# Moving one of the two buffer places of h by 64 bytes in SBUF: attention and SwiGLU on one core

## The chip, the cores and the metric

The kernel runs on one core of one Trainium2 chip. The metric is the device time of one execution in microseconds, the median of several runs.

## The reference

Block-causal attention over 8 batches, 8 heads, 576 positions and a head width of 64, followed by a gated feed-forward layer over the 4608 tokens that come out of it:

```
scores = q @ k^T / sqrt(64), masked by blocks of 64, softmax over keys
x      = (softmax @ v) as [4608, 512]
g      = x @ w_gate                # 512 -> 1536
h      = g * sigmoid(g) * (x @ w_val)
out    = h @ w_out                 # 1536 -> 512
```

## The kernel before, in words

TensorE multiplies in the float32r format. So that nothing of float32 is lost, each operand is kept as two parts, a high one (rounded) and a low one (what the rounding left), and each product is three matmuls: high by high, high by low, low by high.

The feed-forward layer goes over 18 tiles of 256 tokens, and in each over 6 pairs of 128-wide blocks of the 1536 hidden values. A pair has an "up" group and a "down" group:

- up (L1105 to L1107): 48 matmuls into PSUM tiles `gv`. The gate weights (blocks in turn `g_even`, `g_odd`) and the value weights (`v_all`) are the stationary operand, loaded as 128 columns; the parts of x (`xhl`) stream as 256 columns. Of the 48, 12 use `g_even`, 12 `g_odd` and 24 `v_all`.
- between: ScalarE's tanh (L1139), two VectorE products (L1142, L1147), which leave h in `t`; then the high part of h is written by ScalarE (L1152) and the low part by VectorE (L1155), both into `hhl`.
- down (L1197 to L1199): 12 matmuls into `po` or `at`. Here the parts of h in `hhl` are the stationary operand, 128 columns a load, and w_out's parts stream as 512 columns. Those parts are read back from DRAM into `wo` for most tiles; in the first two tiles some of w_out still stands in `g_even`, `g_odd` and `v_all`, from before these are filled with gate and value weights, each row of 512 cut into four pieces of 128.

```
nc.tensor.matmul(o, lhsT=hi[:, d], rhs=xhi[:, 0:w], ...)   # L1105, up: weights loaded, x streams
nc.tensor.matmul(po, lhsT=hi, rhs=whi, ...)                # L1197, down: h loaded, w_out streams
nc.tensor.matmul(po, lhsT=hi, rhs=wlo, ...)                # L1198
nc.tensor.matmul(po, lhsT=lo, rhs=whi, ...)                # L1199
```

`hhl` has two places, `hhl0` and `hhl1`, each with a high and a low tile of 2 KB a partition. A planner in the kernel (`in_order`) goes through all tasks with costs written in the code, gives each its place and fixes the order on every engine. Addresses play no part in it. Attention's matmuls (L442, L569, L653, L782) are put between the groups of the feed-forward.

SBUF tiles get their addresses in the order in which they are made: first the constants, then the weights, then the tags in `first_of`, then the rest when first used. A 64-byte tile `gap`, which nothing reads, stands ahead of `g_even`. In the built program the addresses, modulo 128 bytes, are:

| tiles | role on TensorE | past a multiple of 128 |
|---|---|---|
| `g_odd`, `v_all` | loaded in up; streamed in a few down groups | 64 |
| `g_even` | loaded in up; streamed in a few down groups | 0 |
| `xhl` | streamed in up | 0 |
| `wo` | streamed in down | 0 |
| `hhl0`, `hhl1` | loaded in down | 0 |
| `v`, `parts`, `qk`, `sc`, `t`, `mx` | attention and elementwise work | 0 |

Rows and slices within these tiles begin at multiples of 128 bytes where TensorE reads them.

Of the kernel before, what the change touches and what calls it, by code (L numbers as in the profile page):

```python
# [7 lines left out]
F32 = mybir.dt.float32  # L8
# [10 lines left out]
def kernel(  # L19
# [21 lines left out]
    P = 128  # L41
# [53 lines left out]
    const = ctx.enter_context(tc.tile_pool(name="const", bufs=1))  # L95
# [21 lines left out]
    def tiles_of(tag, place, variant=""):  # L117
        pool, variants = kinds[tag]
        slot = slots[tag][place]
        if slot[0] != variant:  # L120
            shapes, init = variants[variant]
            names = [f"{tag}{place}_{k}" for k in range(len(shapes))]
            slot[:] = variant, [
                x and pool.tile(*x, name=name, tag=name, bufs=1) for x, name in zip(shapes, names)
            ]
            if init:
                init(*slot[1])
        return slot[1]
# [176 lines left out]
    first_of = [("v", ""), ("ob", "signs" if wide else "out"), ("parts", "pair"), ("xhl", ""), ("wo", "raw"), ("hhl", "")]  # L305
    for tag, variant in first_of:
        for place in range(len(slots[tag])):
            tiles_of(tag, place, variant)


    scratch = tiles_of("t", 0)[0]
# [1144 lines left out]
```

## Time and profile before

| what | us |
|---|---|
| median of 3 runs | 1174.53 (1172.72 to 1175.42) |
| the profiled execution: its own time | 1178.6 |
| its span in the trace | 1176.7 |
| TensorE matmul busy | 1149.6, 98% |
| VectorE, ScalarE, GpSimd busy | 746.6, 625.0, 322.1 |

A matmul's record spans from its start to its modelled end, and the next one starts long before that: what a matmul costs in a dense row is the distance from its start to the next start. PE is TensorE's matmuls, PEld its loads of stationary operands. The mean granted clock is 0.991; it is 1.00 after the first 170 us.

### The profile page before, as it was taken

To read this page: it belongs to the slowest core of one execution; us is meant where nothing else is said; L and a number is where in the kernel's file an instruction comes from. 1 tells how busy PE (TensorE), PEld (TensorE's weight loads), DVE (VectorE), ACT (ScalarE), POOL (GpSimd) and SP (SyncE) were. 2 spreads that over 40 slices of the span, in tenths; PEclk is the share of its full clock that TensorE was granted. 3 is DMA by queue.
4 is the path that set the end of the run, shared out by engine and by line. 5 is a ranking of instruction groups with operands and counts; after the bars stand their busy time and mean duration, and the time that the engine had idled before them with its cause. 6 is when DMAs were issued, how large, how long until landed. Compare 5 with 4: busy or idle time off the path is not lost.

```text
span 1176.7 us, 21979 instructions
## 1 busy us (share of the span) xinstructions
PE 1149.6 (98%) x8578; PEld 1029.6 (88%) x8578; DVE 746.6 (63%) x1230; ACT 625.0 (53%) x1114; POOL 322.1 (27%) x139
## 2 busy tenths in 40 slices
PE   6889999999999999999999999999999999999998
PEld 5567878888899998989899998989989898999997
DVE  5798889677678574768567674856648565423222
ACT  5788877646383655637374564637355463212111
POOL 3212100144523333422414332342424233000000
PEclk8899999999999999999999999999999999999999
DMA  7666858756574646755376544745556434654442
GB/s 202 168 169 189 208 178 259 190 175 175 162 180 134 172 143 172 210 176 129 132 201 199 146 150 134 216 140 163 157 161 192 166 108 148 199 160 133 146 166 103
DMA packets 266984, 197.41 MB, mean 168 GB/s; under 512 B 195264, under 2 KB 231376, under 8 KB 266880
## 3 DMA queue, kind: packets, MB, share of 16 engines
q1 hardware_dynamic: 264304, 195.29, 56.8%
q8 instruction: 67, 1.10, 0.4%
q10 hardware_dynamic: 2576, 0.72, 0.3%
q14 instruction: 37, 0.30, 0.1%
HBM read 171.57 MB, written 24.38 MB: 167 GB/s over the span
## 4 chain that ended last, share of the span: by engine, by line
PE 90%; DVE 3%; ACT 3%; DMA 2%; issue 1%; SPq 0%; POOL 0%; ACTq 0%; POOLq 0%; DVEq 0%
PE gv L1105 17%; PE gv L1107 16%; PE gv L1106 16%; PE po L1197 8%; PE po L1198 7%; PE po L1199 7%; PE at L782 7%; PE at L569 5%; PE at L653 1%; PE at L1197 1%; PE at L442 1%; PE at L1198 1%; PE at L1199 1%; DVE mx L710 1%; DMA qk<-in_k_dram 1%
## 5 line engine op out<-in xcount | busy, mean ns | idle before, releaser
L714 POOL PARTITION_ALL_REDUCE mx<-mx x80 | 141.0, 1811 | 441.7 <-DVE mx L710 131.6
L833 POOL PARTITION_ALL_REDUCE mx<-mx x48 | 178.5, 3766 | 229.1 <-DVE mx L710 210.0
L1105 PE MATMUL gv<-xhl,v_all 128*128 128x256 f32 x864 | 241.0, 279 | 0.0
L1107 PE MATMUL gv<-xhl,v_all 128*128 128x256 f32 x864 | 239.2, 277 | 0.0
L1106 PE MATMUL gv<-xhl,v_all 128*128 128x256 f32 x864 | 239.0, 277 | 0.0
L1142 DVE SCALAR_TENSOR_TENSOR t<-t,gv 128x512 f32<-128x512 f32 x108 | 73.8, 684 | 146.6 <-ACT t L1139 146.0
L1105 PEld LDWEIGHTS gv<-xhl,v_all 128*128 128x128 f32 x864 | 162.1, 188 | 3.4 <-issue 2.1
L1106 PEld LDWEIGHTS gv<-xhl,v_all 128*128 128x128 f32 x864 | 162.3, 188 | 0.8
L1155 DVE TENSOR_TENSOR hhl<-t,hhl 128x512 fp32r<-128x512 f32 x108 | 91.4, 847 | 112.3 <-ACT hhl L1152 109.0
L1107 PEld LDWEIGHTS gv<-xhl,v_all 128*128 128x128 f32 x864 | 162.2, 188 | 0.1
L1152 ACT CAST hhl<-t 128x512 fp32r<-128x512 f32 x108 | 67.3, 623 | 156.2 <-PE po L1198 114.4
L1197 PE MATMUL po<-wo,hhl 128*128 128x512 f32 x372 | 148.3, 399 | 0.7 <-ACT ob L1224 0.7
L1198 PE MATMUL po<-wo,hhl 128*128 128x512 f32 x372 | 145.6, 391 | 0.0
L1199 PE MATMUL po<-wo,hhl 128*128 128x512 f32 x372 | 145.3, 390 | 0.0
L738 DVE TENSOR_TENSOR sc<-sc,mx 128x640 f32<-128x640 f32 (+6 forms) x168 | 123.4, 774 | 20.4 <-POOL mx L714 20.4
L1139 ACT ACTIVATE t<-gv 128x512 f32<-128x512 f32 x108 | 64.6, 598 | 119.6 <-PE gv L1107 116.9
L1105 PE MATMUL gv<-xhl,g_even 128*128 128x256 f32 x432 | 124.2, 288 | 0.2 <-DVE t L1142 0.2
L742 ACT ACTIVATE sc<-sc 128x1024 f32<-128x1024 f32 (+3 forms) x104 | 105.8, 1030 | 32.5 <-DVE sc L738 31.4
L1106 PE MATMUL gv<-xhl,g_even 128*128 128x256 f32 x432 | 122.5, 283 | 0.0
L1107 PE MATMUL gv<-xhl,g_even 128*128 128x256 f32 x432 | 122.3, 283 | 0.0
L1105 PE MATMUL gv<-xhl,g_odd 128*128 128x256 f32 x432 | 120.4, 279 | 0.0
L1107 PE MATMUL gv<-xhl,g_odd 128*128 128x256 f32 x432 | 119.5, 277 | 0.4 <-DVE g_odd L986 0.4
(175 smaller groups left out, 2398.8 us busy)
## 6 DMA issues: line engine op xcount, KB each, us to landing
wo<-wo_d SPq DMA_DIRECT2D x200, 512.0 KB
out_dram<-ob SPq DMA_DIRECT2D x35, 256.0 KB
v<-in_v_dram SPq DMA_DIRECT2D x64, 128.0 KB
xt<-x_d SPq DMA_DIRECT2D x64, 128.0 KB
rt<-r_d SPq DMA_DIRECT2D x128, 64.0 KB
qk<-in_q_dram SPq DMA_DIRECT2D x112, 72.0 KB
qk<-in_k_dram SPq DMA_DIRECT2D x104, 72.0 KB
x_d<-xu SPq DMA_DIRECT2D x24, 288.0 KB
```

What stands on the lines that cost most here:

```text
L714: nc.gpsimd.partition_all_reduce(m, m, channels=P, reduce_op=bass_isa.ReduceOp.max)
L738: nc.vector.tensor_tensor(piece(c), scores_of(c), m, ALU.subtract)
L742: nc.scalar.activation(x, x, AF.Exp)
L782: nc.tensor.matmul(ps[0][own(x), 1 - i if sums else i, q0 - s0 : s1 - s0], lhsT=ones if sums else vt[0][:, 2 * lane + c, own(x)], rhs=sc[0 ...
L833: nc.gpsimd.partition_all_reduce(m, m, channels=P, reduce_op=bass_isa.ReduceOp.add)
L1105: nc.tensor.matmul(o, lhsT=hi[:, d], rhs=xhi[:, 0:w], start=first, stop=False)
L1106: nc.tensor.matmul(o, lhsT=hi[:, d], rhs=xlo[:, 0:w], start=False, stop=False)
L1107: nc.tensor.matmul(o, lhsT=lo[:, d], rhs=xhi[:, 0:w], start=False, stop=last)
L1155: nc.vector.tensor_tensor(hh[1][:, 0:n], t[0][:, 0:n], hh[0][:, 0:n].bitcast(F32), ALU.subtract)
L1197: nc.tensor.matmul(po, lhsT=hi, rhs=whi, start=i + y == 0, stop=False)
L1198: nc.tensor.matmul(po, lhsT=hi, rhs=wlo, start=False, stop=False)
L1199: nc.tensor.matmul(po, lhsT=lo, rhs=whi, start=False, stop=i + y == NFC - 1)
```

## The change

A 64-byte tile that nothing reads is made between the two places of `hhl`, and another behind them:

```
     for tag, variant in first_of:
         for place in range(len(slots[tag])):
+            if tag == "hhl" and place:
+                const.tile([P, 16], F32, name="gap1")
             tiles_of(tag, place, variant)
+    const.tile([P, 16], F32, name="gap2")
```

`hhl0` stays at 156160 and 158208, multiples of 128. `hhl1` goes from 160256 and 162304 (multiples of 128) to 160320 and 162368 (64 bytes past one). Everything made later (`t`, `qk`, `mx`, `sc`, `sr`, `xt`, `xu`, `st`, `rt`) moves by 128 bytes, so it keeps its place within 128 bytes; what began at a multiple of 256 now begins 128 bytes past one. All instructions of the program stay the same and in the same order on every engine, with the same semaphores; only addresses differ. 636 of the 1296 down matmuls load from `hhl1`: 612 of them stream `wo`, 24 stream `v_all`.

## The prediction

> **What bounds the kernel.** I read the page first, for which engine is full and which one makes up the chain that ended last, then TensorE's waits and its busy time from 170 us on.
>
> ```profile
> PE 1149.6 (98%) x8578; PEld 1029.6 (88%) x8578; DVE 746.6 (63%) x1230; ACT 625.0 (53%) x1114; POOL 322.1 (27%) x139
> PE 90%; DVE 3%; ACT 3%; DMA 2%; issue 1%; SPq 0%; POOL 0%; ACTq 0%; POOLq 0%; DVEq 0%
> ```
> ```profile
> 170.00:1177.00 1007.00, 1001.53 (x7431) 914.57 (x7429) 610.13 (x961) 494.33 (x870) 283.97 (x99) 1.00 0.56 165
> ```
> ```profile
> PE po L1197 <- ACT ob L1224: 0.7, 2, 0.3
> PE at L848 <- ACT xu L797: 0.6, 1, 0.6
> PE gv L1105 <- DVE t L1142: 0.2, 1, 0.2
> ```
>
> The first line gives busy time and share by engine, the second the shares of the chain. The third is the stretch from 170 us to the end: after its length come the busy times of PE (1001.5 of 1007), PEld, DVE, ACT and POOL, the granted clock (1.00) and the DMA share (0.56). The last three are all the waits of PE that the profile finds in that stretch, 1.5 us together. So from 170 us on the kernel is one dense row of matmuls, and of the 636 that the change touches all but some 30 lie there. A matmul whose start-to-start distance grows by a nanosecond lengthens the kernel by a nanosecond; nothing stands in front to hide it. The question is only what an address does to a matmul's distance.
>
> **What the trace shows of addresses.** In the up groups the streamed operand begins at a multiple of 128 bytes. Two of the loaded operands begin 64 bytes past one, and `g_even` at one. By tile, L1107's instructions (columns: minimum, median and maximum duration in ns):
>
> ```profile
> L1107 PE MATMUL gv<-xhl,v_all x864: 276/276/388, 60.6 to 1167.3; 128*128 128x256 f32 x173
> L1107 PEld LDWEIGHTS gv<-xhl,g_even x432: 187/192/330, 28.7 to 1163.1; 128*128 128x128 f32 x144
> L1107 PE MATMUL gv<-xhl,g_even x432: 274/283/415, 28.8 to 1163.2; 128*128 128x256 f32 x144
> L1107 PEld LDWEIGHTS gv<-xhl,g_odd x432: 186/188/193, 59.0 to 1164.4; 128*128 128x128 f32 x144
> L1107 PE MATMUL gv<-xhl,g_odd x432: 276/276/384, 59.1 to 1164.6; 128*128 128x256 f32 x144
> ```
> And one such group late in the kernel, in order of time (start, duration); each group is 12 matmuls long:
>
> ```profile
> 1010.47 0.28 PE L1105 MATMUL gv<-xhl,g_even 128*128 128x256 f32 x1
> ...
> 1011.90 0.28 PE L1105 MATMUL gv<-xhl,g_odd 128*128 128x256 f32 x1
> ...
> 1013.26 0.28 PE L1105 MATMUL gv<-xhl,v_all 128*128 128x256 f32 x1
> ```
>
> With `g_even` 12 matmuls take 1.43 us, 119 ns each; with `g_odd` 1.36 us, 113 ns each. Same shape, same streamed data: where load and stream begin alike modulo 128, a matmul of 256 columns costs 6 to 7 ns more, and the loads are 4 ns longer. So an operand load and the stream beside it do disturb each other here, and the 64 bytes matter.
>
> That would promise a gain for the down groups, where all of `hhl` and `wo` begin alike. But there the stream is twice as long, and the rows say something else. A whole down group of 12 with `wo` (loaded and streamed both at multiples of 128):
>
> ```profile
> 1007.72 0.40 PE L1197 MATMUL po<-wo,hhl 128*128 128x512 f32 x1
> ...
> 1009.11 0.39 PE L1197 MATMUL po<-wo,hhl 128*128 128x512 f32 x1
> ```
>
> It ends where the `g_even` row above begins: 2.75 us for 12, 229.2 ns each. The first six take 1.39 us (231.7 each), the last six 1.36 (226.7 each, twice the 113.3 of an undisturbed 256 columns). So a group starts with a disturbance and settles into none after five or six matmuls, though both operands begin alike.
>
> The early part has the opposite case: w_out's parts streamed from `g_odd` or `v_all`, 64 bytes past, against `hhl` at a multiple of 128. That is the combination that the change makes of `hhl1` and `wo`, with the roles exchanged.
>
> ```profile
> L1198 PE MATMUL po<-wo,hhl x372: 387/389/402, 171.7 to 1133.9; 128*128 128x512 f32 x186
> L1198 PE MATMUL po<-g_even,hhl x4: 389/394/395, 86.1 to 161.4; 128*128 128x512 f32 x4
> L1198 PE MATMUL po<-g_odd,hhl x4: 393/394/398, 87.5 to 163.9; 128*128 128x512 f32 x4
> L1198 PE MATMUL po<-v_all,hhl x4: 394/396/400, 104.8 to 118.7; 128*128 128x512 f32 x4
> ```
> ```profile
> 87.25 0.39 PE L1197 MATMUL po<-g_odd,hhl 128*128 128x512 f32 x1
> ...
> 88.66 0.25 PE L416 MATMUL at<-ident,qk 96*128 96x96 f32 x1
> ```
> ```profile
> 104.55 0.40 PE L1197 MATMUL po<-v_all,hhl 128*128 128x512 f32 x1
> ...
> 105.96 0.28 PE L1105 MATMUL gv<-xhl,g_odd 128*128 128x256 f32 x1
> ```
> ```profile
> 160.51 0.40 PE L1197 MATMUL po<-g_even,hhl 128*128 128x512 f32 x1
> ...
> 161.21 0.39 PE L1197 MATMUL po<-g_even,hhl 128*128 128x512 f32 x1
> ...
> 161.88 0.28 PE L1105 MATMUL gv<-xhl,v_all 128*128 128x256 f32 x1
> ...
> 162.24 0.40 PE L1197 MATMUL at<-v_all,hhl 128*128 128x512 f32 x1
> ...
> 164.34 0.28 PE L1105 MATMUL gv<-xhl,v_all 128*128 128x256 f32 x1
> ```
>
> Six matmuls from 87.25 take 1.41 us, 235 ns each, though six with `g_even` ran ahead of them, so that a start-up disturbance should have settled. Six from 104.55 take 1.41 us, 235 each. Nine from 162.24 take 2.10 us, 233.3 each, to the ninth. The control is the run from 160.51 with `g_even`, both at multiples of 128, in the same crowded stretch: three in 0.70 us (233), then three in 0.67 (223 by these rounded starts), so it settles. Against 64 bytes the distance stays at about 233, and the shortest duration with `v_all` (394) lies above the median with `wo` (389). Hence the forecast: in the down groups the 64 bytes do harm, not good.
>
> **The change part by part.**
>
> - Removed: the settled state of the 612 matmuls that load `hhl1` and stream `wo`, 229.2 ns each on average with their start.
> - Put in its place: the distance of the rows with 64 bytes between. Ends: 233.3 (the longest run) and 235 (the runs of six); all 21 together are (1.41 + 1.41 + 2.10) / 21 = 234.3. I take 233.7, nearer to the longest run, since the runs of six stand in the first 110 us beside work that late groups do not have. 233.7 - 229.2 = 4.5 ns, times 612 = 2.75 us. The ends give 2.5 and 3.5 us.
> - The 24 matmuls that load `hhl1` and stream `v_all` now begin alike: 24 x -4.5 ns = -0.1 us.
> - The bound on the other side: all 612 at the undisturbed 226.7 from the first on, 612 x -2.5 ns = -1.5 us.
> - Writing `hhl1` (ScalarE, VectorE), the two unused tiles, the planner: nothing. No instruction is added or moved, and these engines are 53% and 63% busy beside a PE that waits 1.5 us for all of them after 170 us. If the writes got slower by some ns, that slack would take it.
> - The 128 bytes by which `qk`, `sc`, `t`, `mx` and the others move: I take 0, since load and stream keep their distance modulo 128. Where what counts is a larger period, the nearest rows are these, 240 matmuls with `qk` streamed:
>
> ```profile
> L569 PE MATMUL at<-qk,parts x240: 192/297/392, 319.4 to 960.4; 128*128 128x288 f32 x40, 128*128 128x448 f32 x40, 128*128 128x320 f32 x40
> L569 PE MATMUL at<-parts,parts x240: 273/295/369, 319.5 to 960.5; 128*128 128x288 f32 x40, 128*128 128x448 f32 x40, 128*128 128x320 f32 x40
> ```
>
> At the price of `g_even`'s loads, 7 ns either way, 240 of them are worth 1.7 us at the most, a bound for the range and no term.
>
> Sum: 2.75 - 0.1 = +2.7 us. The profiled execution took 1178.6 us (span 1176.7 and 1.9 around it), 4 us above the median of the runs, 1174.53; on it the sum is 1181.3, on the median 1177.2, +0.23%.
>
> **A rule against the trace.** The row first: `g_even`'s 283 against `g_odd`'s 276. The Trainium skill, "TensorE: Matmul & The Clock Gate", section "Step-by-step: what each phase is for", says that TensorE has two independent read ports into SBUF, and that loading the next weights takes no read bandwidth from the running matmul. By that rule no address changes anything, and the time would stay at 1174.5. The trace disagrees by 7 ns a matmul; but it has no row with `wo` against a load 64 bytes off, so the rule's result stays a rival.
>
> **The rivals.**
>
> 1. *Nothing happens.* A load of 128 columns beside a stream of 512 has room, and the state settles whatever the address. For it: the last six of the group at 1007.72 show no cost though both begin alike; the early rows with 64 bytes stand in a stretch with more DMA and a kept, four-piece w_out. Against it: `g_even`'s kept pieces are cut the same way, and settle. 1174.5 us.
> 2. *The other side: the sign of the up groups holds.* With 64 bytes between, the start of each group is undisturbed too, and a down group of `hhl1` takes 12 x 226.7 ns. This decides if the first six of such a group fall from 1.39 to 1.36 us: -1.5 us, 1173.0. Against it stand the 21 early matmuls.
> 3. *The 128 bytes behind it.* The pieces of q and k land 128 bytes off a multiple of 256, and at the start TensorE waits for them:
>
> ```profile
> 2.24 3.01 DMA qk<-in_k_dram
> 5.27 4.68 DMA qk<-in_k_dram
> ```
>
> These are pieces of the chain, 7.7 us; if they took half as long again (no row gives a size), that would be +3.8 us, 1178.3 alone and 1181.0 with the forecast. The rows of L569 give up to 1.7 us, of either sign. Behind the start DMA hides beside PE, as the waits show. The Trainium skill, "DMA: Bandwidth & Descriptors", section "How a descriptor splits into AXI transactions", has a piece off a 256-byte boundary pay for more beats, for a 256-byte piece 12 in place of 8 by my estimate from that page; no run here shows it for a write into SBUF.
>
> That the change does not do what it says is excluded: the addresses of the built program are 64 bytes off.
>
> **How the numbers follow.** The forecast has 0.62, with its own range 1176.3 to 1178.6; rival 1 has 0.16, rival 2 0.12, rival 3 0.10. About 0.2%, 2.35 us, is what a measurement of this kernel can tell from no change, and the forecast's 2.7 lies just above it: two thirds of its chance count as slower (0.42), one third as the same (0.20). Rival 1 is the same; rival 2 is mostly the same (0.09) and rarely faster (0.03). Rival 3 is split, 0.06 slower and 0.04 faster; 0.01 from rival 1 goes to faster, for noise. Together: faster 0.08, the same 0.44, slower 0.48. The range goes from rival 2's end to the forecast's upper end and a little into rival 3: 1172.9 to 1179.0.
>
> **What would show it.** Right: in down groups that load `hhl1` late in the kernel, twelve matmuls take about 2.80 us in place of 2.75, with durations of 393 to 398 ns to the last, so that the median of L1198 with `wo` splits into 389 and about 395; groups of `hhl0` stay at 2.75. `g_even`'s 283 and `g_odd`'s 276 stay. Rival 1: all groups keep 2.75. Rival 2: groups of `hhl1` take 2.72, without the long start. Rival 3: `qk`'s first landings or L569's durations differ. What would make it wrong is that the early rows owe their 233 to something else than the 64 bytes: the crowded stretch, or the way in which the kept w_out is cut.

## The result and the profile after

The changed kernel takes 1178.38 us (median of 20 runs) against 1175.51 for the kernel before in the same comparison: ratio 1.0021, 95% interval 1.0014 to 1.0029, so 1.6 to 3.4 us slower. The forecast was 1177.2, 2.7 us above its base; the medians differ by 2.9. The profiled execution alone does not show it: its span is 1176.6 us, before 1176.7, because the stretch up to the 1300th matmul (the first 193 us, with parts at a lower granted clock: 0.94 on average in the first 170 us before, 0.95 after) happened to be 1.9 us shorter. From that matmul to the last the trace has 981.2 us against 979.4.

The page's first line, then by line and shape (busy us, mean ns):

```profile
PE 1151.8 (98%) x8578; PEld 1030.4 (88%) x8578; DVE 746.7 (63%) x1230; ACT 623.9 (53%) x1114; POOL 322.4 (27%) x139
```
```profile
L1201 PE MATMUL po<-wo,hhl x372: 388/393/398, 170.0 to 1133.7; 128*128 128x512 f32 x186
```

PE is 2.2 us busier, the other engines stand where they were. L1201 (L1198 before) had a median of 389 with `wo`; now it is 393, since half its rows load `hhl1`. Two neighbouring down groups, in order of time, first `hhl0`, then `hhl1` (start, duration; the last row of each is the start of the next group):

```profile
998.96 0.40 PE L1200 MATMUL po<-wo,hhl 128*128 128x512 f32 x1
...
1000.34 0.39 PE L1200 MATMUL po<-wo,hhl 128*128 128x512 f32 x1
...
1001.70 0.28 PE L1108 MATMUL gv<-xhl,g_even 128*128 128x256 f32 x1
```
```profile
1007.22 0.39 PE L1200 MATMUL po<-wo,hhl 128*128 128x512 f32 x1
1007.44 0.40 PE L1201 MATMUL po<-wo,hhl 128*128 128x512 f32 x1
1007.68 0.39 PE L1202 MATMUL po<-wo,hhl 128*128 128x512 f32 x1
1007.91 0.40 PE L1200 MATMUL po<-wo,hhl 128*128 128x512 f32 x1
...
1009.77 0.40 PE L1202 MATMUL po<-wo,hhl 128*128 128x512 f32 x1
1010.01 0.28 PE L1108 MATMUL gv<-xhl,g_even 128*128 128x256 f32 x1
```

`hhl0`: 1.38 us for six, 1.36 for the other six, 2.74 together; it settles as before. `hhl1`: 2.79 us. Its first matmul is undisturbed (226 ns to the next start, where a group of `hhl0` has 233); then 236 and 231 alternate to the end. Over all groups that stream `wo` the mean distance is 232.8 ns for `hhl1` (229.15 before) and 228.9 for `hhl0`. These means, and those of the runs below, leave out distances above 245 ns, where the next matmul came late.

### The profile page after: what moved, and what is told of

The parts are those of the page before. It is cut to its first block, busy times and chain, and to the rows that moved or that the text cites. A ratio compares the mean times of both kernels' runs of the same rounds, so it can differ in the third digit from the quotient of the medians.

```text
span 1176.6 us, 21979 instructions
## 1 busy us (share of the span) xinstructions
PE 1151.8 (98%) x8578; PEld 1030.4 (88%) x8578; DVE 746.7 (63%) x1230; ACT 623.9 (53%) x1114; POOL 322.4 (27%) x139
## 4 chain that ended last, share of the span: by engine, by line
PE 88%; DVE 4%; ACT 4%; DMA 3%; issue 1%; SPq 1%; POOL 0%; DVEq 0%; POOLq 0%; ACTq 0%
PE gv L1108 16%; PE gv L1110 16%; PE gv L1109 16%; PE po L1200 8%; PE po L1201 7%; PE po L1202 7%; PE at L785 7%; PE at L572 5%; DMA wo<-in_moe_w_out_dram 2%; PE at L656 1%; DVE mx L713 1%; PE at L1200 1%; PE at L1201 1%; ACT sc L463 1%; PE at L1202 1%
## 5 line engine op out<-in xcount | busy, mean ns | idle before, releaser
L1158 DVE TENSOR_TENSOR hhl<-t,hhl 128x512 fp32r<-128x512 f32 x108 | 90.9, 842 | 113.3 <-ACT hhl L1155 109.9
L1201 PE MATMUL po<-wo,hhl 128*128 128x512 f32 x372 | 146.4, 393 | 0.0
L1110 PE MATMUL gv<-xhl,g_odd 128*128 128x256 f32 x432 | 119.6, 277 | 0.4 <-DVE g_odd L989 0.4
```

What stands on the lines that cost most here:

```text
L1110: nc.tensor.matmul(o, lhsT=lo[:, d], rhs=xhi[:, 0:w], start=False, stop=last)
L1158: nc.vector.tensor_tensor(hh[1][:, 0:n], t[0][:, 0:n], hh[0][:, 0:n].bitcast(F32), ALU.subtract)
L1201: nc.tensor.matmul(po, lhsT=hi, rhs=wlo, start=False, stop=False)
```

## The experiments

Three theories at first. A: what counts is the distance in bytes between the loaded block and the stream. B: a 64-byte offset of either one. C: the 128 bytes by which everything behind `hhl` moved. Each diff is against the kernel before.

**Both places of h moved** (`both64`), **`wo` moved alone** (`wo64`), **both moved together** (`wohhl64`), **only the shift behind** (`shift128`).

The lines that each adds (shortened, names left out):

```
both64:  + const.tile([P, 16], F32)   # ahead of hhl0, and one more behind hhl1
wo64:    + const.tile([P, 16], F32)   # ahead of wo0 and again ahead of hhl0; hhl then 128 past a multiple of 256
wohhl64: + const.tile([P, 16], F32)   # ahead of wo0 alone, so that wo and hhl both stand at 64; one more behind hhl1
shift128:+ const.tile([P, 32], F32)   # behind hhl1
```

> Both places of h's parts begin 64 bytes past a multiple of 128, w_out's parts (wo) at one. Theory A (what counts is whether load and stream begin alike modulo 128, and 512 columns pay where they do not): hhl0's late groups turn to 236, 231, 236, 231 ns like hhl1's in the changed kernel, 2.79 to 2.80 us for twelve in place of 2.75; the cost doubles, +4.5 to +5 us on the kernel before, about +0.4%. Theory C (the cost comes from the 128 bytes by which everything behind moves): as the changed kernel, +2.5 us, with hhl0 groups at 2.75.

> The streamed side is moved in place of the loaded one: wo begins 64 bytes past a multiple of 128, both places of h at one. Theory A: the same as with both places of h moved, +4 to +5 us, twelve matmuls of a late group 2.79 to 2.80 us, both places alike, though the start of a group may keep its 233. Theory B (the loaded operand's own address decides, whatever the stream's): 0, groups stay at 2.75.

> wo and both places of h begin 64 bytes past a multiple of 128, so load and stream are alike again, and h's first load runs beside xhl, which is 64 bytes off. Theory A: groups settle at 226.7, and the start of a group after an up group is undisturbed too: 2.72 to 2.75 us for twelve; 0 to -2.5 us on the kernel before. Theory B: as with both places moved, +4.5 us.

> Nothing is moved within 128 bytes: a tile of 128 bytes behind h's places alone moves qk, sc, t and the others, as the change does. Theory A: 0, at most -0.5 us from groups that follow L569 (in the changed kernel those of hhl0 start with 250, 227, 227 in place of 254, 224, 231, 236). Theory C: +2.5 us.

Measured: `both64` 1180.9 us, 1.0036 (1.0023 to 1.0049); `wo64` 1182.82, 1.0058 (1.0046 to 1.0071); `wohhl64` 1176.79, 1.0003 (0.9994 to 1.0012); `shift128` 1176.34, 0.9998 (0.999 to 1.0007). L1198 by tile, in this order of the first three:

```profile
L1198 PE MATMUL po<-wo,hhl x372: 388/396/399, 169.6 to 1136.0; 128*128 128x512 f32 x186
```
```profile
L1198 PE MATMUL po<-wo,hhl x372: 388/394/399, 168.0 to 1137.2; 128*128 128x512 f32 x186
```
```profile
L1198 PE MATMUL po<-wo,hhl x372: 387/390/403, 170.6 to 1133.0; 128*128 128x512 f32 x186
```

Medians 396 and 394 where load and stream are 64 bytes apart, 390 where both are moved and so stand alike. Doing the change to both places about doubles its price. B and C fall, A holds. What A does not give is that `wo64` costs 2 us more than `both64`: its up groups are slower by some 3 us, though no operand of theirs moved. The run `hhl1_192` below shows where they lose it.

**Another distance in the change's place** (`hhl1_32`: the gap ahead of `hhl1` is 32 bytes).

> As the change, but h's second place begins 32 bytes past a multiple of 128. Theory A in its narrow form (64-byte pieces in turn in two halves, so 32 off is partly in each): late hhl1 groups between 2.72 and 2.79 us, 0 to +1.2 us on the kernel before. In its wide form (any distance that is no multiple of 128 costs as 64 does): 2.79 us, +2.2 us.

1179.31 us, 1.0023 (1.0015 to 1.0032), mean distance of `hhl1` 233.7 ns: 32 bytes cost what 64 do. The median of L1198 is 395, both places together:

```profile
L1198 PE MATMUL po<-wo,hhl x372: 388/395/398, 169.4 to 1134.4; 128*128 128x512 f32 x186
```

**Harvesting the rule in the up groups** (`geven64`: the old `gap` behind `g_even`, so that all weights begin 64 bytes past a multiple of 128, off the stream; `all_best`: that and `wohhl64`).

> The unused tile that stands ahead of g_even is made behind it: all gate and value weights begin 64 bytes past a multiple of 128, xhl, wo and h's parts at one. Theory A (256 columns cost 113.3 ns where load and stream stand 64 bytes apart, 120 where alike): g_even's twelve matmuls fall from 1.43 to 1.36 us like g_odd's; 1296 x 5.8 ns = -7.5 us on the kernel before, about -0.64%. Theory D (g_even is slow because it is the first weight after a down group, wherever it begins): 0.

> As with g_even moved, and wo and both places of h 64 bytes past a multiple of 128 too (alike with each other, 64 apart from xhl). Theory A: -7.5 us from g_even; the down groups settle at 226.7 as with wo and h moved together, which alone made no difference that could be told: 0 to -1.5 us more. Theory D: 0.

Misses, both: 1185.46 us, 1.0079 (1.0066 to 1.0093), and 1189.19, 1.0108 (1.009 to 1.0125). L1107 of `geven64`:

```profile
L1107 PE MATMUL gv<-xhl,v_all x864: 276/280/415, 58.8 to 1173.9; 128*128 128x256 f32 x173
L1107 PE MATMUL gv<-xhl,g_even x432: 276/280/416, 28.8 to 1169.7; 128*128 128x256 f32 x144
L1107 PE MATMUL gv<-xhl,g_odd x432: 276/280/416, 57.5 to 1171.1; 128*128 128x256 f32 x144
```

`g_even` went from 283 to 280, but `g_odd` and `v_all`, which did not move, went from 276 to 280 (113.6 and 114.0 ns apart to 117.5). Distance alone cannot do that. Theory F: the pace is a cycle into which load and stream fall, and the matmuls ahead decide which one.

**Nothing but matmuls** (`micro`, `micro2`; they leave out the whole computation and time rows of alike matmuls at set distances; in `micro2` a row of 256 columns follows no, three or twelve matmuls at distance 0, these behind twelve of 512 columns).

> The kernel's whole computation is left out. After 120 matmuls to warm up it runs rows of 48 matmuls that depend on nothing but their order: 128 columns loaded, 512, 448, 384, 320, 256, 192 or 128 streamed from a tile at a multiple of 128 bytes, the loaded tile 0, 32, 64, 96 or 128 bytes past one (five lines of the source). Nothing else runs beside them. Theory A: at 256 columns 120 ns a matmul at 0 and 128, 113 at 64; at 512 columns 226.7 at 0 and 128, 233 at 64; 0 and 128 alike at every width; the widths between show where the sign turns. Theory E (other engines or DMA beside the matmuls cause the difference): no width depends on the offset.

> The kernel's whole computation is left out. Rows of 36 matmuls of 512 or 256 columns, the loaded tile 0, 64, 128, ... 448 bytes past a multiple of 512 (eight lines), the stream at one. Ahead of each row stand 12 matmuls of 512 columns at distance 0; then, for the rows named none, nothing more, for three and twelve 3 or 12 matmuls of 256 columns at distance 0. Theory F (the pace is a cycle that load and stream fall into, so what ran ahead counts beside the distance; it is to explain that g_odd and v_all, not moved, went from 113.5 to 117.6 ns when g_even was moved): at 448 (the distance of g_odd and v_all from xhl), 117 to 118 ns in the row none and 113.3 in the row twelve. Theory A (the distance alone decides): the three rows of one distance are alike. At 512 columns both expect 226.7 at 0 and about 233 at 64 and 448.

The pages sort rows by busy time, the last but one number is the mean duration in ns. `micro`, 512 columns, distances 0 (L45), 32 (L48), 64 (L51), 96 (L54) and 128 (L57); then `micro2`, 512 columns at 0 (L50), 64 (L52), 128 (L54), 192 (L56) and 256 (L58), and 256 columns at 192 (L56) without (`none`) and with three at distance 0 ahead:

```profile
L54 PE MATMUL ps<-stream,load 128*128 128x512 f32 x48 | 11.4, 396 | 0.0
L51 PE MATMUL ps<-stream,load 128*128 128x512 f32 x48 | 11.4, 396 | 0.0
L48 PE MATMUL ps<-stream,load 128*128 128x512 f32 x48 | 11.4, 395 | 0.0
L57 PE MATMUL ps<-stream,load 128*128 128x512 f32 x48 | 11.3, 395 | 0.0
L45 PE MATMUL ps<-stream,load 128*128 128x512 f32 x48 | 11.1, 389 | 0.0
```
```profile
L52 PE MATMUL none<-stream,load 128*128 128x512 f32 x36 | 8.6, 396 | 0.0
...
L54 PE MATMUL none<-stream,load 128*128 128x512 f32 x36 | 8.5, 395 | 0.0
L56 PE MATMUL none<-stream,load 128*128 128x512 f32 x36 | 8.4, 391 | 0.0
...
L50 PE MATMUL none<-stream,load 128*128 128x512 f32 x36 | 8.3, 389 | 0.0
L58 PE MATMUL none<-stream,load 128*128 128x512 f32 x36 | 8.3, 389 | 0.0
...
L56 PE MATMUL none<-stream,load 128*128 128x256 f32 x36 | 4.4, 279 | 0.0
...
L56 PE MATMUL three<-stream,load 128*128 128x256 f32 x36 | 4.2, 276 | 0.0
```

At 512 columns a start-to-start distance of 226.7 ns at 0 becomes 233.4 at 64, 232.4 at 128 and 229.0 at 192; 256 is as 0, and 320, 384 and 448 repeat 64, 128 and 192, so the period is 256 bytes. No DMA and no other engine is needed for it. Theory A's other figures were missed: 128 is not as 0, and at 256 columns no distance of `micro` gives 113 (117.4 to 119.6). How much the distance matters goes by the width: at 320 columns 146.5 to 146.8 ns, at 192 and 128 columns 111.0 to 111.7. At 256 columns the distance 192 runs at 117.8 ns by itself, but at 113.3 for all 36 behind three or twelve matmuls at distance 0; a row at distance 0 settles at 120 itself. In the kernel `g_odd` and `v_all` stand at 192 behind twelve of `g_even` at 0: the slow `g_even` sets the pace of the 36 behind it. That is what `geven64` took away.

**F against "every distance but 0 costs the same"** (`hhl1_192`: a gap of 192 bytes ahead of `hhl1`).

> h's second place begins 192 bytes past a multiple of 256 instead of 64; wo and h's first place stay at multiples of 256. Theory F (a period of 256 bytes, as the loop of nothing but matmuls showed: 229.0 ns at distance 192 and 512 columns, 233.4 at 64): 612 x (229.0 - 229.15) = about 0, no change within 0.1%, and hhl1's late groups stay at 2.75 us. Rival (every distance but 0 costs what 64 does): groups of 2.80 us and +2.2 us, +0.2%.

1180.23 us, 1.0032 (1.0019 to 1.0045). In the down groups F is right: 229.14 ns, as before. In the time it misses, since the price stands behind them. After a late `hhl1` group, the starts of `g_even`, of `g_odd` and of the next down group:

```profile
908.22 0.28 PE L1105 MATMUL gv<-xhl,g_even 128*128 128x256 f32 x1
...
909.66 0.28 PE L1105 MATMUL gv<-xhl,g_odd 128*128 128x256 f32 x1
...
913.90 0.40 PE L1197 MATMUL po<-wo,hhl 128*128 128x512 f32 x1
```

The 36 matmuls from 909.66 take 4.24 us, 117.8 ns each, not 113.3. So it is in 20 of the 29 full up groups (48 matmuls in a row, from 193 us on) behind a down group of `hhl1`, and in none of the 34 behind one of `hhl0`. What a down group leaves behind carries through all twelve of `g_even`, and then they no longer set the pace. `g_odd` and `v_all` together are 3.1 us longer.

`wo64` shows the same: in 17 of those 63 groups the last 36 matmuls run at 117.8, which makes 2.7 us of what its up groups lose. One of them, from its `g_odd` to the next down group, 4.24 us:

```profile
904.41 0.28 PE L1105 MATMUL gv<-xhl,g_odd 128*128 128x256 f32 x1
...
908.65 0.39 PE L1197 MATMUL po<-wo,hhl 128*128 128x512 f32 x1
```

**Using it** (`first3`, `first6`: `g_even` becomes two tiles; the blocks of a group's first three or six matmuls stay at distance 0, the rest are 192 bytes off).

```
-    g_even = [const.tile(half_w, F32R, name=f"g_even{x}") for x in range(2)]
+    g_even[0][0] = const.tile([P, 1, DFF // 2], F32R, name="g_even0a")             # at 0; first6: [P, 2, ...]
+    const.tile([P, 48], F32, name="gap_a")
+    for x in range(2):
+        g_even[x][1] = const.tile([P, NDC - 1, DFF // 2], F32R, name=f"g_even{x}b")  # at 192; first6: NDC - 2
+    const.tile([P, 16], F32, name="gap_b")
+    g_even[1][0] = const.tile([P, 1, DFF // 2], F32R, name="g_even1a")             # at 0
...
```

> h's two places and wo as in the kernel before. g_even is two tiles: the blocks of its first three matmuls of a group stay alike with xhl (distance 0), the blocks of the other nine are 192 bytes off, as g_odd's are. Theory F (three alike matmuls set the pace that the 192 ones then keep at 113.3): 9 of 12 gate matmuls go from 120 to 113.3 and the g_odd ones stay at 113.6, 972 x 6.5 ns = -6.3 us, less an estimate of 1 to 1.5 us for some 18 more early matmuls that the split asks for: -4.5 to -6 us, -0.4 to -0.5%, faster than both kernels. Rival (three are not enough, or the pace goes by the distance alone): as with all of g_even moved, 117.5 throughout and +9 us.

> As with three alike matmuls ahead, but six: g_even's blocks of the first six matmuls of a group alike with xhl (distance 0), the other six 192 bytes off. Theory F: six are enough also behind the attention's matmuls, where three were not (those groups ran at 117.7 throughout, 14 of them), since before's groups there show the alike pace of 120 from the fourth matmul on. So no group of 117.7 behind the attention, and 6 of a group's 12 gate matmuls at 113.3 in place of 120: 594 x 6.5 ns = -3.9 us, plus an estimate of 1 us for the split early matmuls: -3 us, -0.25%. Rival (what sets the pace is not these matmuls but the work ahead of a group): the groups behind the attention stay at 117.7, and the time is within 0.1% of before, as with three.

`first3`: 1175.62 us, 1.0007 (0.9983 to 1.003), no difference that can be told and so a miss: most groups do as F says (mean 114.4 ns for `g_even`'s twelve, 113.3 for the rest), but three are too few behind attention: there 13 of 14 groups of 48 run the rest at 117.7. `first6`: 1174.57, 0.9987 (0.9976 to 0.9998), faster by 1.6 us, half of the 3 expected. Such a group of `first3`, from its `g_odd` to its end, then the same of `first6`:

```profile
934.20 0.28 PE L1125 MATMUL gv<-xhl,g_odd 128*128 128x256 f32 x1
...
938.43 0.30 PE L588 MATMUL at<-qk,parts 128*128 128x288 f32 x1
```
```profile
935.01 0.28 PE L1125 MATMUL gv<-xhl,g_odd 128*128 128x256 f32 x1
...
939.09 0.30 PE L588 MATMUL at<-qk,parts 128*128 128x288 f32 x1
```

4.23 us against 4.08 for the same 36 matmuls. With six, 13 of the 14 groups settle at 113.3. After the first 193 us `g_even` gains 3.5 us in the trace, and `g_odd` and `v_all` give back 2.2: 1.4 in eleven up groups, some of them short, that keep 117.8, and 0.8 in one late start at 206 us, where TensorE waits for VectorE's `t`. Net of that the trace is 1.2 us shorter, the medians 1.6. The rule is used with a gain of 0.13% whose interval ends at 0.02%, not with the 0.25% expected.

## Why the prediction was right, point by point

- *A denser matmul row is paid in full.* Right: nothing hides it. `hhl1`'s groups are 2.1 us longer, and the time follows. That the sum's 2.7 lies so near to the 2.9 between the medians is in part luck: after the first 193 us the two traces differ by 1.8 us, of which the down groups make 2.0, attention's matmuls 0.4, `g_even` -0.4 and `v_all` -0.2. The interval of 1.6 to 3.4 us holds 1.8 as well as 2.9; no row shows the rest.
- *4.5 ns for each of 612 matmuls.* Right in sign, too large: 232.8 - 229.15 = 3.6 ns, 2.2 us in place of 2.75. The early rows with w_out in the old tiles do stand at the same distance of 64 (load less stream, modulo 256), but 233.7 left out that the first of a group escapes (226). That is the part of rival 2 that came true; the other eleven refute it.
- *`g_even` stays.* By its median, yes:

```profile
L1108 PE MATMUL gv<-xhl,g_even x432: 277/283/582, 29.1 to 1162.8; 128*128 128x256 f32 x144
```

Behind `hhl1` groups it is quicker, by 0.3 us in all. The sum has no such term: it took a matmul's cost for its own, where it also depends on what went ahead.
- *What counts is modulo 128.* Wrong: the period is 256. `g_odd` stands at 192 and the change at 64, so the up groups' sign (rival 2) could not have been carried over. The 24 with `v_all`, of which the sum says that they come to stand alike, stand 128 apart by that period, which costs 232.4 ns at 512 columns in `micro2`; the term of 0.1 us is too small to be seen. And `g_even`'s extra 7 ns were not a loss to be mended but what buys the 36 behind it 113.3 instead of 117.5.
- *Nothing happens.* Refuted by `both64` and `wohhl64` in the kernel and by `micro` without it. Rows that differ in one address have 226.7 against 233.4 ns. The rule of the Trainium skill, "TensorE: Matmul & The Clock Gate", section "Step-by-step: what each phase is for", that the next load takes no read bandwidth from the running matmul, does not agree with that.
- *The shift behind.* 0, as taken: `shift128` has 0.9998. L569's matmuls take 0.4 us more there and 0.3 in the changed kernel.

What inside the chip makes the cycles is open: the runs show the period of 256 bytes and the memory of the pace, not their cause.

## What to carry to other kernels

In a row of float32r matmuls without gaps, with loads of 128 columns as here, the distance between the loaded block and the stream in SBUF, modulo 256 bytes, is worth up to 3% of a 512-column matmul; keep them alike there, and move both or neither. Judge a layout by the groups that follow too: a matmul that looks slow by its address may be setting the pace of those behind it, and in `geven64` taking 2.3 us from `g_even` cost 13 us in the matmuls behind it. A row of one kernel at a given distance holds only with the same history.

## What was not expected of the hardware

The pace has a memory: in `micro2` three matmuls at distance 0 make the next 36, at distance 192, run at 113.3 ns instead of 117.8. It carries across line, width and PSUM target: in 20 of 29 groups of `hhl1_192` from a down group of 512 columns through twelve of 256 into the 36 behind them.
